# One narrowing operation per slot with its addition on GpSimd, three products held over into a new phase, and the sums' low halves two units later

## The chip, the cores and the metric

One core of a Trainium2 chip runs the whole program. The metric is the device time of one execution in microseconds. The engines are named as in the profile: PE (TensorE) with its weight loads (PEld), DVE (VectorE), ACT (ScalarE), POOL (GpSimd), and SP's queue, which issues every transfer.

## The reference

Windowed attention, then a mixture of eight experts with all experts applied to all tokens, then a two-layer network. Everything is float32.

```python
def reference(q, k, v, w_gate, w1, w2, w_in, w_out):
    x = attention(q, k, v)                    # (2304, 512), banded masks
    P = exp(x @ w_gate - max)                 # (2304, 8)
    for _ in range(8):                        # rows, then columns to equal sums
        P /= P.sum(1, keepdims=True) + 1e-9
        P /= P.sum(0, keepdims=True) + 1e-9
        P *= 2304 / 8
    y = sum(P[:, e:e+1] * (relu(x @ w1[e]) @ w2[e]) for e in range(8))   # hidden 1024
    r = relu(y @ w_in)                        # hidden 2048
    return (r * r) @ w_out
```

## The kernel before, in words

Every float32 operand is split into a high and a low half, and a product is three matmuls: high by high, low operand by high, high by low. The attention fills the first 117 us. After it comes a list of 80 steps of 256 hidden columns each, in four phases: steps 0 to 31 are the experts for a pair of 512-token blocks plus a single 256-token block, steps 32 to 63 the experts for a second pair, steps 64 to 71 the two-layer network for the first pair and the single block, steps 72 to 79 for the second pair. The list `first` holds 0, 32, 64 and 72.

In a step the first layer of the pair is seven units u1 to u7 (`l1_pair`), a seven-product scheme for a two-by-two block product: `blk` slots hold blocks of the weights and `sum` slots hold their sums, made on POOL. A unit is 6 matmuls of 512 columns. u2, u4, u5 and u7 read the sums, u2 as the first, and its third matmul is the first to read their low half. The banks of PSUM are `s`, `pt`, `xt` for the first layer and three `mm` banks for the rest. u5 and u6 write into bank `pt` that ACT has just copied out of (lines 570 and 574); u7 writes into `xt` that DVE has just added from (line 575).

The second layer of step i-1 runs inside step i: `l2_units` makes eight units of 6 matmuls of 512 columns for the pair, and for the single block four units of 6 matmuls of 256 columns (two of 512 in the last network). Each takes an `mm` bank, and DVE adds the bank to `acc` (line 647) before the bank can be used again three units later. `l1_single` makes two more units for the single block.

The order of a step is written by hand: u1 to u4; then second layer, u5, second layer, u6, second layer, u7; then the other five second-layer units; then those of the single block; then the single block's first layer. So a step has 21 units in the first phase and 15 in the second and fourth. At the start of a phase (`first[1:]`) all second-layer units of the old phase run ahead, and u1 to u7 of the new one follow without any between them.

`after(k, f)` puts work on ACT, DVE, POOL or SP's queue behind the unit that is k units from here; every engine takes its work in the order in which it is written. `prep_w(i)` makes the next step's weights in this way: POOL's four additions for the sums at units 0 and 1 (lines 144 to 149), the high half of the sums on ACT at unit 10, their low half (`suml`, line 135) on DVE at unit 12, the low halves of `w2` and `blk` on DVE at units 3 and 5, each followed on SP's queue by the load of the next weights.

The weights of the last network arrive as 64-bit floats. `narrow` turns them into 32-bit floats with bit operations, 32 pieces in all: a load into a buffer `xb`, seven operations on DVE between that buffer and a second one, a store to DRAM. It is a generator, and `narrow_on()` takes it to its next `yield`. It is called from steps 5 to 29 after units 0 and 8, and from steps 33 to 58 after units 0, 5 and 10. The two `xb` buffers are used again by the next piece.

Of the kernel before, what the change touches and what calls it, by code (L numbers as in the profile page):

```python
# [9 lines left out]
F32 = mybir.dt.float32  # L10
# [4 lines left out]
ALU = mybir.AluOpType  # L15
# [26 lines left out]
SCALED = 3  # L42
# [5 lines left out]
def tile_kernel(ctx: ExitStack, tc: tile.TileContext, a):  # L48
    nc = tc.nc
    out = a["out"]  # L50
# [35 lines left out]
    def bank(tag):  # L86
        return psum.tile([128, 512], F32, tag=tag, name=tag, bufs=bufs[tag])
# [9 lines left out]
    sums = wts.tile([128, 4, 256], F32, name="sums")  # L97
# [15 lines left out]
    def load_w(i, which):  # L113
        if i >= len(steps):
            return
        dst = raw1.rearrange("p b c -> p (b c)") if which == 0 else raw2
        nc.sync.dma_start(dst, src_w(i, which))
# [5 lines left out]
    def prep_w(i):  # L123

        out = []
        tt = nc.gpsimd.tensor_tensor
        c = lambda z, k: z[:, k, :]
        flat = lambda z: z.rearrange("p b c -> p (b c)")

        def hi(w, src):  # L130
            return lambda: nc.scalar.copy(w[0], src)  # L131

        def lo(w, src, then=lambda: None):
            def f():
                nc.vector.tensor_tensor(out=w[1], in0=src, in1=w[0].bitcast(F32), op=ALU.subtract)  # L135
                then()

            return f

        if i + 1 < len(steps):  # L140
            w = wset[(i + 1) % 2]

            def s1():
                tt(out=c(sums, 0), in0=c(raw1, 2), in1=c(raw1, 3), op=ALU.add)  # L144
                tt(out=c(sums, 2), in0=c(raw1, 0), in1=c(raw1, 2), op=ALU.subtract)

            def s2():
                tt(out=c(sums, 1), in0=c(sums, 0), in1=c(raw1, 0), op=ALU.subtract)
                tt(out=c(sums, 3), in0=c(raw1, 1), in1=c(sums, 1), op=ALU.subtract)

            out += [(0, s1), (1, s2), (2, hi(w["blk"], flat(raw1)))]
            out += [(5, lo(w["blk"], flat(raw1), lambda: load_w(i + 2, 0)))]
            out += [(10, hi(w["sum"], flat(sums))), (12, lo(w["sum"], flat(sums)))]
        if i >= 0:
            w = wset[i % 2]
            out += [(1, hi(w["w2"], raw2)), (3, lo(w["w2"], raw2, lambda: load_w(i + 1, 1)))]
        return out

    def xb():
        return post[0].tile([128, 2 * T], F32, tag="xb", name="xb", bufs=2)  # L160

    def narrow(which, s, k):

        n = 512
        src = xb().bitcast(I32).rearrange("p (n w) -> p n w", w=2)
        cols = slice(2 * n * k, 2 * n * k + 2 * n)
        nc.sync.dma_start(
            src.rearrange("p n w -> p (n w)"), a["w_in" if which == 0 else "w_out"][s].bitcast(I32)[:, cols]
        )
        yield  # L170
        low, high = src[:, :, 0], src[:, :, 1]
        topf = xb()[:, :n]
        top = topf.bitcast(I32)
        nc.vector.tensor_scalar(
            out=top, in0=high, scalar1=3, scalar2=0x3FFFFFFF,
            op0=ALU.logical_shift_left, op1=ALU.bitwise_and,
        )
        nc.vector.scalar_tensor_tensor(
            out=top, in0=high, scalar=-0x40000000, in1=top, op0=ALU.bitwise_and, op1=ALU.bitwise_or
        )  # L180
        yield
        nc.vector.tensor_scalar(
            out=high, in0=high, scalar1=0x7FFFFFFF, scalar2=None, op0=ALU.bitwise_and
        )
        nc.vector.scalar_tensor_tensor(
            out=topf, in0=high, scalar=float(0x38100000), in1=topf, op0=ALU.is_ge, op1=ALU.mult
        )
        yield
        nc.vector.tensor_scalar(
            out=high, in0=top, scalar1=-0x800000, scalar2=None, op0=ALU.bitwise_and  # L190
        )
        nc.vector.scalar_tensor_tensor(
            out=low.bitcast(F32), in0=low.bitcast(U32), scalar=2.0**-52, in1=high.bitcast(F32),
            op0=ALU.mult, op1=ALU.mult,
        )
        nc.vector.tensor_tensor(out=topf, in0=topf, in1=low.bitcast(F32), op=ALU.add)
        nc.sync.dma_start(w32[which, s, :, n * k:n * k + n], topf)
        yield

# [64 lines left out]
    def load_ps(e):  # L264
        if e < E:
            p = p_t[e] = post[0].tile([128, NSG], F32, tag="ps", name="ps", bufs=1)
            spread(p, e, SINGLE)
# [193 lines left out]
    first = [0, NS1, 2 * NS1, 2 * NS1 + NS2]  # L461

    def phase(i):
        return max(k for k in range(4) if first[k] <= i)

    def pair_of(i):
        return phase(i) % 2
# [16 lines left out]
    def after(k, f):  # L484

        due.setdefault(clock[0] + k, []).append(f)

    def run(u):
        u()
        for f in due.pop(clock[0], []):  # L490
            f()
        clock[0] += 1
# [98 lines left out]
    def l1_single(i):  # L591
        def unit(fc):
            if fc == 0:
                g_t[i, 1] = tuple(
                    post[0].tile([128, FC, NSG], F32R, tag=n, name=n, bufs=1) for n in ("sgh", "sgl")
                )
            gh, gl = g_t[i, 1]
            ps = bank("mm")[:, :NSG]
            hi, lo = wset[i % 2]["blk"]
            k = 0  # L600
            for kc in range(KC):
                c = slice((4 * fc + kc) * 128, (4 * fc + kc) * 128 + 128)
                for w, z in ((hi, xs_hi), (hi, xs_lo), (lo, xs_hi)):
                    nc.tensor.matmul(ps, w[:, c], z[:, kc], start=k == 0, stop=k == 3 * KC - 1)  # L604
                    k += 1
            p = p_t[steps[i][1] // SPE] if steps[i][0] and i >= SCALED else None
            evac_g(i, gh[:, fc], gl[:, fc], ps, p, 0)
            s = steps[i][1]
            if fc == FC - 1 and steps[i][0] and s % SPE == SPE - 1:
                after(1, lambda: load_ps(s // SPE + 1))  # L610

        return [lambda fc=fc: unit(fc) for fc in range(FC)]
# [48 lines left out]
    def operands(i):  # L661

        if phase(i) == 1:
            return new_operands(x_dram)
        t0 = PAIRS[pair_of(i)]
        return new_operands(y_dram[:, :, t0:t0 + 2 * T])

    def operands_single():
        z = xb().rearrange("p (k n) -> p k n", n=NSG)
        nc.sync.dma_start(z, y_dram[:, :, SINGLE:SINGLE + NSG])  # L670
        return single_pieces(z)
# [3 lines left out]
    with tc.manual_schedule():  # L675
# [148 lines left out]
        done = [0]  # L824

        def narrow_on():
            done[0] += 1
            next(narrows, None)

        def settled(i):  # L830

            while done[0] % 4:
                narrow_on()

        for i in range(len(steps) + 1):
            l2 = l2_units(i - 1, 0)
            l2s = l2_units(i - 1, 1)
            if i == len(steps):
                for u in l2 + l2s:
                    run(u)  # L840
                break
            if i in first[1:]:
                for u in l2 + l2s:
                    run(u)
                l2, l2s = [], []
            l1 = l1_pair(i) if i else first_units
            order = l1[:4] if i else l1[2:4]
            for u in l1[4:]:
                order += l2[:1] + [u]
                l2 = l2[1:]  # L850
            order += l2 + l2s
            if i == first[2]:
                l1s = l1_single(i)
                order = l1[:1] + l1s[:1] + l1[1:2] + l1s[1:] + l1[2:]
            elif pair_of(i) == 0:
                order += l1_single(i)
            for k, f in prep_w(i):
                after(min(k, len(order) - 1), f)
            if i + 2 in first[1:]:
                settled(i)  # L860
                for k, f in operands(i + 2):
                    after(len(order) + k, f)
            if i == first[2] - 4:
                for _ in narrows:
                    pass
                for k, f in enumerate(operands_single()):
                    after(8 + 2 * k, f)
            slow = i + 2 in first or i + 1 in first or i in first
            for k, u in enumerate(order):
                run(u)  # L870
                if i < SCALED:
                    next(sink, None)
                if SCALED + 2 <= i < first[2] - 5 and not slow and k in ((0, 8), (0, 5, 10))[pair_of(i)]:
                    narrow_on()
        settle()

# [82 lines left out]
```

## Time and profile before

| | us |
|---|---|
| median of 3 runs | 2045.76 |
| the runs | 2044.92 to 2049.02 |
| the profiled execution | 2052.68 |
| its span from first to last instruction | 2050.9 |
| PE busy | 2017.1 (98%) |
| DVE busy | 1558.3 (76%) |
| ACT busy | 720.4 (35%) |
| POOL busy | 386.6 (19%) |

Matmuls are pipelined and their ends are modelled, so the busy time of PE also covers small gaps. The distance between the starts of two matmuls shows more: 0.23 us at 512 columns and 0.12 us at 256 where nothing is in the way.

### The profile page before, as it was taken

How to read it: one execution, taken by the hardware profiler on the slowest of the kernel's cores; microseconds unless marked ns; L12 is line 12 of the kernel's file. 1: busy time of each engine (PE TensorE's matmuls, PEld its weight loads, DVE VectorE, ACT ScalarE, POOL GpSimd, SP SyncE). 2: the span in 40 equal slices, each digit the busy share in tenths (PEclk: the TensorE clock that was granted, in tenths of full speed). 3: DMA queues.
4: the chain of work that ended last, by engine and by line, in shares of the span. 5: the costliest groups of instructions: out<-in, count | busy, mean ns of one | idle time of the engine just before them, and what ended most of it. 6: DMA issues, size and time to landing. Idle time of an engine off the chain costs nothing.

```text
span 2050.9 us, 28660 instructions
## 1 busy us (share of the span) xinstructions
PE 2017.1 (98%) x11584; PEld 1663.0 (81%) x11584; DVE 1558.3 (76%) x2435; ACT 720.4 (35%) x1149; POOL 386.6 (19%) x416
## 2 busy tenths in 40 slices
PE   9999999999999999999999999999999999999999
PEld 7778888888888888888888888888888878887887
DVE  4766777777777777778888888888887786678676
ACT  3443222223322232223433333333333344344542
POOL 3522311111011111111311212121211231123120
PEclk8899999999999999999999999999999999999999
DMA  8512121222212121213222322323221231112111
GB/s 279 177 65 61 52 57 57 62 65 62 65 50 61 56 61 47 70 57 98 103 93 87 87 85 71 97 78 98 82 86 59 75 111 42 39 54 103 62 42 52
DMA packets 71509, 159.35 MB, mean 78 GB/s; under 512 B 6336, under 2 KB 33104, under 8 KB 71376
## 3 DMA queue, kind: packets, MB, share of 16 engines
q1 hardware_dynamic: 71376, 157.52, 23.8%
q8 instruction: 91, 1.49, 0.3%
q14 instruction: 42, 0.34, 0.1%
HBM read 137.49 MB, written 20.00 MB: 77 GB/s over the span
## 4 chain that ended last, share of the span: by engine, by line
PE 87%; DVE 10%; ACT 2%; issue 1%; POOL 0%; ACTq 0%; DVEq 0%; POOLq 0%
PE mm L635 42%; PE pt L477 16%; PE s L477 10%; PE xt L477 9%; PE mm L604 5%; DVE acc L647 3%; PE xt L349 2%; DVE gl L511 2%; DVE g L525 1%; DVE suml L135 1%; PE mm L752 1%; PE s L297 1%; PE pt L334 1%; DVE x_lo L212 1%; DVE s L584 1%
## 5 line engine op out<-in xcount | busy, mean ns | idle before, releaser
L647 DVE TENSOR_TENSOR acc<-mm,acc 128x512 f32<-128x512 f32 x746 | 473.2, 642 | 188.4 <-PE mm L635 184.4
L635 PE MATMUL mm<-gl,w2h 128*128 128x512 f32 x1024 | 403.3, 394 | 0.0
L635 PE MATMUL mm<-gh,w2h 128*128 128x512 f32 x1024 | 402.3, 393 | 0.8 <-DVE acc L647 0.7
L635 PE MATMUL mm<-gh,w2l 128*128 128x512 f32 x1024 | 402.8, 393 | 0.0
L533 ACT CAST gh<-g 128x512 fp32r<-128x512 f32 x308 | 191.5, 622 | 592.8 <-DVE g L525 592.6
L144 POOL TENSOR_TENSOR sums<-raw 128x256 f32<-128x256 f32 x80 | 66.2, 827 | 1466.7 <-DVE suml L135 1423.8
L635 PEld LDWEIGHTS mm<-gh,w2h 128*128 128x128 f32 x1024 | 192.4, 188 | 46.8 <-DVE acc L647 1.6
L635 PEld LDWEIGHTS mm<-gl,w2h 128*128 128x128 f32 x1024 | 192.3, 188 | 43.9
L635 PEld LDWEIGHTS mm<-gh,w2l 128*128 128x128 f32 x1024 | 192.3, 188 | 43.7
L511 DVE TENSOR_TENSOR gl<-g,gh 128x512 fp32r<-128x512 f32 x308 | 223.8, 731 | 0.9 <-ACT gh L533 0.9
L525 DVE SCALAR_TENSOR_TENSOR g<-s,pp 128x512 f32<-128x512 f32 x183 | 128.8, 704 | 111.6 <-PE s L477 109.4
L477 PE MATMUL pt<-x_hi,sumh 128*128 128x512 f32 x320 | 126.4, 395 | 3.7 <-ACT s L570 3.7
L477 PE MATMUL s<-x_hi,blkh 128*128 128x512 f32 x320 | 126.3, 395 | 1.0 <-ACT pt L558 1.0
L477 PE MATMUL xt<-x_hi,sumh 128*128 128x512 f32 x320 | 126.6, 396 | 0.0
L477 PE MATMUL xt<-x_lo,sumh 128*128 128x512 f32 x320 | 126.0, 394 | 0.0
L477 PE MATMUL pt<-x_lo,sumh 128*128 128x512 f32 x320 | 125.9, 393 | 0.0
L477 PE MATMUL xt<-x_hi,suml 128*128 128x512 f32 x320 | 125.9, 393 | 0.0
L477 PE MATMUL pt<-x_hi,suml 128*128 128x512 f32 x320 | 125.8, 393 | 0.0
L477 PE MATMUL s<-x_lo,blkh 128*128 128x512 f32 x320 | 125.8, 393 | 0.0
L477 PE MATMUL s<-x_hi,blkl 128*128 128x512 f32 x320 | 125.5, 392 | 0.0
L135 DVE TENSOR_TENSOR w2l<-raw,w2h 128x1024 fp32r<-128x1024 f32 x80 | 100.7, 1259 | 14.9 <-ACT w2h L131 14.9
L533 ACT CAST sgh<-g 128x256 fp32r<-128x256 f32 x74 | 29.9, 406 | 219.0 <-DVE g L525 219.0
(151 smaller groups left out, 3970.3 us busy)
## 6 DMA issues: line engine op xcount, KB each, us to landing
raw<-in_w SPq DMA_DIRECT2D x128, 512.0 KB, 3.5
raw<-w SPq DMA_DIRECT2D x32, 512.0 KB, 3.4
v<-in_v SPq DMA_DIRECT2D x24, 384.0 KB, 3.9
pp<-p_dram SPq DMA_DIRECT2D x32, 256.0 KB, 5.6
xb<-in_w_in SPq DMA_DIRECT2D x16, 512.0 KB, 4.7
w<-xb SPq DMA_DIRECT2D x32, 256.0 KB, 2.3
xb<-in_w_out SPq DMA_DIRECT2D x16, 512.0 KB, 4.7
k<-in_k SPq DMA_DIRECT2D x24, 224.0 KB, 4.6
```

Of the source, the lines that this page charges most:

```text
L135: nc.vector.tensor_tensor(out=w[1], in0=src, in1=w[0].bitcast(F32), op=ALU.subtract)
L144: tt(out=c(sums, 0), in0=c(raw1, 2), in1=c(raw1, 3), op=ALU.add)
L212: return lambda: nc.vector.tensor_tensor(out=x_lo[:, k, j], in0=z, in1=x_hi[:, k, j].bitcast(F32), op=ALU.subtract)
L297: nc.tensor.matmul(ps[QB * head:QB * head + QB, 2 * (g % 3) + g // 3, :], qt[rows, pr, g * QB:g * QB + QB], kt[rows, pr, g * QB:g * QB + K ...
L349: nc.tensor.matmul(xt[D * h:D * h + D, pr, c * QB:c * QB + QB], vt[keys, c, head * D:head * D + D], pt[keys, c * 128 + head * QB:c * 128 + ...
L477: nc.tensor.matmul(ps, w[:, c], z[:, x, j], start=start and k == 0, stop=stop and k == 5, skip_group_check=True)
L511: nc.vector.tensor_tensor(out=glo, in0=z, in1=ghi.bitcast(F32), op=ALU.subtract)
L525: nc.vector.scalar_tensor_tensor(out=held["g"], in0=src, scalar=0.0, in1=held["r"], op0=ALU.max, op1=ALU.mult)
L533: after(k + 1, lambda: nc.scalar.copy(ghi, held["g"]))
L604: nc.tensor.matmul(ps, w[:, c], z[:, kc], start=k == 0, stop=k == 3 * KC - 1)
L635: nc.tensor.matmul(ps, lhsT, rhs, start=k == 0, stop=k == 3 * FC - 1)
L647: nc.vector.tensor_tensor(out=dst, in0=ps, in1=dst, op=ALU.add)
```

## The change

- The low half of the sums is put on DVE behind unit 14 of a step, not 12. Where a step has only 15 units that is its last one.
- `narrow` yields after each operation, so one call is one operation, and a piece is eight calls instead of four: the load; six operations on DVE, one a call; the addition with the store.
- The last of its seven operations, the addition, goes to POOL.
- `narrow_on()` is called five times a step: after units 0, 1, 2, 7 and 20 in the first phase, after 0, 1, 2, 7 and 13 in the second.
- At the start of a phase the last three second-layer units of the old phase are kept back and put between u5, u6 and u7 of the new one.
- In step 0 the two units of the single block go between u4, u5 and u6.

```diff
-            out += [(10, hi(w["sum"], flat(sums))), (12, lo(w["sum"], flat(sums)))]
+            out += [(10, hi(w["sum"], flat(sums))), (14, lo(w["sum"], flat(sums)))]
...
             op0=ALU.logical_shift_left, op1=ALU.bitwise_and,
         )
+        yield
         nc.vector.scalar_tensor_tensor(
...
             out=high, in0=high, scalar1=0x7FFFFFFF, scalar2=None, op0=ALU.bitwise_and
         )
+        yield
...
             out=high, in0=top, scalar1=-0x800000, scalar2=None, op0=ALU.bitwise_and
         )
+        yield
...
-        nc.vector.tensor_tensor(out=topf, in0=topf, in1=low.bitcast(F32), op=ALU.add)
+        yield
+        nc.gpsimd.tensor_tensor(out=topf, in0=topf, in1=low.bitcast(F32), op=ALU.add)
         nc.sync.dma_start(w32[which, s, :, n * k:n * k + n], topf)
...
-            while done[0] % 4:
+            while done[0] % 8:
...
+            ahead = []
             if i in first[1:]:
-                for u in l2 + l2s:
-                    run(u)
-                l2, l2s = [], []
+                ahead, l2, l2s = l2[:-3] + l2s, l2[-3:], []
             l1 = l1_pair(i) if i else first_units
-            order = l1[:4] if i else l1[2:4]
-            for u in l1[4:]:
-                order += l2[:1] + [u]
-                l2 = l2[1:]
-            order += l2 + l2s
-            if i == first[2]:
-                l1s = l1_single(i)
-                order = l1[:1] + l1s[:1] + l1[1:2] + l1s[1:] + l1[2:]
-            elif pair_of(i) == 0:
-                order += l1_single(i)
+            l1s = l1_single(i) if pair_of(i) == 0 else []
+            if i == 0:
+                order = l1[2:4] + l1s[:1] + l1[4:5] + l1s[1:] + l1[5:]
+            elif i == first[2]:
+                order = l1[:1] + l1s[:1] + l1[1:2] + l1s[1:] + l1[2:4]
+            else:
+                order = l1[:4]
+            if i:
+                for u in l1[4:]:
+                    order += l2[:1] + [u]
+                    l2 = l2[1:]
+                order += l2 + l2s
+                if i != first[2]:
+                    order += l1s
+            for u in ahead:
+                run(u)
...
-                if SCALED + 2 <= i < first[2] - 5 and not slow and k in ((0, 8), (0, 5, 10))[pair_of(i)]:
+                if SCALED + 2 <= i < first[2] - 5 and not slow and k in ((0, 1, 2, 7, 20), (0, 1, 2, 7, 13))[pair_of(i)]:
                     narrow_on()
```

## Rows read from the trace of the kernel before

**Rows 1.** Busy time of each engine, page of the whole execution.
```profile
PE 2017.1 (98%) x11584; PEld 1663.0 (81%) x11584; DVE 1558.3 (76%) x2435; ACT 720.4 (35%) x1149; POOL 386.6 (19%) x416
```

**Rows 2.** Busy time by stretch: steps 11, 12, 30, 41 and 43, u1 to u1.
```profile
407.59:434.27 26.68, 26.68 (x140) 22.61 (x139) 18.98 (x31) 7.91 (x12) 3.31 (x4) 1.00 0.16 50
434.27:461.82 27.55, 27.00 (x140) 22.72 (x139) 20.60 (x34) 7.91 (x12) 3.31 (x4) 1.00 0.23 73
922.60:949.07 26.47, 26.47 (x140) 22.60 (x139) 21.06 (x34) 7.91 (x12) 3.33 (x4) 1.00 0.30 100
...
1170.30:1191.12 20.82, 20.82 (x91) 16.91 (x90) 17.77 (x27) 7.05 (x10) 3.35 (x5) 1.00 0.22 70
1211.92:1232.91 20.99, 20.99 (x91) 16.83 (x90) 18.90 (x29) 7.05 (x10) 4.58 (x5) 1.00 0.31 101
```

**Rows 3.** Waits of PE, whole execution: total us, times, longest.
```profile
PE mm L635 <- DVE acc L647: 11.3, 31, 1.4
...
PE pt L477 <- ACT s L570: 3.7, 6, 0.7
PE pt L477 <- ACT s L574: 2.4, 4, 0.7
```

**Rows 4.** Timeline of PE in step 32: start, us; u6 after u5.
```profile
999.53 0.39 PE L477 MATMUL pt<-x_hi,suml 128*128 128x512 f32 x1
1000.60 0.50 PE L477 MATMUL pt<-x_hi,blkh 128*128 128x512 f32 x1 [0.68 <-ACT s L574]
1000.93 0.39 PE L477 MATMUL pt<-x_lo,blkh 128*128 128x512 f32 x1
```

**Rows 5.** Timeline of PE in step 12: first matmuls of single-block units 16, 17, 18.
```profile
456.11 0.38 PE L635 MATMUL mm<-sgh,w2h 128*128 128x256 f32 x1 [0.17 <-DVE acc L647]
...
457.48 0.39 PE L635 MATMUL mm<-sgh,w2h 128*128 128x256 f32 x1 [0.38 <-DVE acc L647]
...
458.29 0.28 PE L635 MATMUL mm<-sgh,w2h 128*128 128x256 f32 x1
```

**Rows 6.** Timeline of DVE in steps 12 and 61, and 62 beginning.
```profile
454.24 1.22 DVE L135 TENSOR_TENSOR suml<-sums,sumh 128x1024 fp32r<-128x1024 f32 x1
...
1605.31 0.69 DVE L647 TENSOR_TENSOR acc<-mm,acc 128x512 f32<-128x512 f32 x1
1605.91 1.22 DVE L135 TENSOR_TENSOR suml<-sums,sumh 128x1024 fp32r<-128x1024 f32 x1
...
1607.65 0.85 DVE L511 TENSOR_TENSOR gl<-g,gh 128x512 fp32r<-128x512 f32 x1
```

**Rows 7.** Timeline of PE, steps 61 and 62: start of unit 13, u1, u2's third matmul.
```profile
1605.11 0.40 PE L635 MATMUL mm<-gh,w2h 128*128 128x512 f32 x1
...
1607.91 0.40 PE L477 MATMUL s<-x_hi,blkh 128*128 128x512 f32 x1
...
1609.77 0.40 PE L477 MATMUL xt<-x_hi,suml 128*128 128x512 f32 x1
```

**Rows 8.** Groups by form (busy us, mean ns); POOL's timeline, step 61.
```profile
L196 DVE TENSOR_TENSOR xb<-xb 128x512 f32<-128x512 f32 x32 | 24.7, 773 | 1.1
...
L144 POOL TENSOR_TENSOR sums<-raw 128x256 f32<-128x256 f32 x80 | 66.2, 827 | 1466.7 <-DVE suml L135 1423.8 <-DMA raw<-in_w 42.9
L206 POOL TENSOR_TENSOR xb<-xb 128x512 f32<-128x512 f32 x24 | 33.9, 1412 | 67.6 <-DVE x_lo L212 66.6
...
1607.90 1.19 POOL L145 TENSOR_TENSOR sums<-raw 128x256 f32<-128x256 f32 x1
```

**Rows 9.** Transfers: issues, KB each, median us to landing.
```profile
xb<-in_w_in SPq DMA_DIRECT2D x16, 512.0 KB, 4.7
```

**Rows 10.** Timeline of DVE in step 45: three operations back to back.
```profile
1261.98 1.22 DVE L135 TENSOR_TENSOR blkl<-raw,blkh 128x1024 fp32r<-128x1024 f32 x1
1263.11 0.42 DVE L174 TENSOR_SCALAR xb<-xb 128x512 int32<-128x512 int32 x1
1263.57 0.69 DVE L178 SCALAR_TENSOR_TENSOR xb<-xb 128x512 int32<-128x512 int32 x1
```

## Prediction

> **What bounds the kernel now.** The page says PE: busy 98% of the span, DVE 76% [rows 1]. An average hides where the rest goes, so the table by stretch comes next. In the second phase a step takes 20.8 us, one in four 21.0, and PE is busy in all of it [rows 2]: no edit can gain there but what a few short stalls hold. In the first phase steps alternate: 26.68 us, 27.55 us, and in step 30, which has no narrowing, 26.47 us [rows 2]. The work on PE is the same, so 0.2 or 1.1 us of a step is waiting. The list of PE's waits names it: 11.3 us in 31 waits for DVE's addition out of an `mm` bank, and 6.1 us in 10 waits for ACT's copies out of `pt` [rows 3]. The timeline gives the price of such a wait: u6 starts 1.07 us after the matmul before it and the next one 0.33 us on, where two times 0.23 would do (2.80 us for twelve [rows 7]). The loss is 0.94 us for an idle time of 0.68, so 0.26 on top of each wait, 0.10 of it the slower restart [rows 4].
>
> Why the waits are there: in step 12 the single block's units come every 0.71 us, and DVE, with 2 us of narrowing behind unit 8 and the sums' low half (1.22 us) behind unit 12, is late with the banks of units 13 and 14. Unit 17 starts 1.37 us after unit 16 in place of 0.71 [rows 5, 6].
>
> **The change part by part.** Gains first.
>
> *Narrowing one operation at a time, first phase.* None of the five spots lies between unit 7 and the last unit. The 12 heavier steps (27.55) lose their DVE queue and would come to 26.47: 12 x 1.08 = 13.0 us; the 13 lighter ones 13 x 0.21 = 2.7.
>
> *The sums' low half at unit 14, first phase.* It now stands between the additions of units 14 and 15. Count from the start of unit 15. DVE's addition starts 0.20 us after the unit's end (1605.11 to 1605.31 [rows 6, 7]) and the next operation follows 0.60 later, so the low half runs from 0.80, the next operation 1.13 later (the 1024-column row [rows 10]) at 1.93, and bank 15 is free at about 2.40. Unit 18 needs that bank at 3 x 0.71 = 2.13. That costs 0.27 + 0.10 = 0.37 us in each of 27 steps: 10.0. The two lines together: 13.0 + 2.7 - 10.0 = 5.7. Some old stalls behind unit 12, before the phase changes, get shorter because the additions of units 13 and 14 now come 1.1 us sooner (steps 3, 31, 63, 71; the longest of their waits is 1.4 [rows 3]); I take 3 us, bounds 0 and 5.
>
> *Three products kept for the new phase.* u5 and u6 then have a unit of 1.4 us in front of each, longer than the 0.94 they lose. Of the 6 and 4 waits in rows 3, three phases hold one of each kind: 3 x 2 x 0.94 = 5.6 us. The other four share 6.1 - 6 x 0.68 = 2.0 us of idle time; two of them are in step 0, where single-block units now stand between: half of it and 0.1 a wait, 1.2. What could take this back is DVE, which in the run ahead has fewer units to catch up in: 0.4.
>
> *Second phase, narrowing.* One step in four loses 0.2 us to it now [rows 2]: six steps, 1.2.
>
> Gains together: 5.7 + 3 + 5.6 + 1.2 - 0.4 + 1.2 = 16.3 us.
>
> *The sums' low half, second and fourth phase.* Here a step has 15 units, so unit 14 is the last and the low half stands behind its addition. From u1 of the next step: addition at 0.20, low half at 0.80, ready at 0.80 + 1.22 = 2.02. PE's first matmul that reads it, u2's third, now starts 1609.77 - 1607.91 = 1.86 after u1 [rows 7]. Before the change it was ready at 1605.91 + 1.22 = 1607.13, 2.6 us ahead of that matmul [rows 6]. Now u2 is held by 0.16 + 0.10 = about 0.3 us a step. And one narrowing operation now stands behind unit 13: unit 13's addition starts at -1.20, `gl` follows at -0.60 and ends its turn at 0.00, and then 0.46 [rows 10] or 0.60 us of narrowing come before the addition of unit 14, so that it starts 0.26 or 0.40 later than 0.20. Of eight calls three are the short kind, three the long kind and two not on DVE: (3 x 0.56 + 3 x 0.70 + 2 x 0.3) / 8 = 0.55 us. The 26 steps with narrowing cost 14.3, the 4 after them and the 6 of the fourth phase 0.3 each, 3.0. Sum 17.3 us. No row shows PE waiting for this tile; from below the price is nothing, if the weights come through sooner than DVE's row ends, from above 0.8 us in each of 36 steps, 29. I take 17.3, since it is made of rows of the same instructions.
>
> *Load, addition and first operation of a piece.* A piece has eight calls and a step five, so in a cycle of eight steps the addition falls once behind unit 0, with the next load behind unit 1 and the first operation behind unit 2 (steps 8, 16, 24 and 36, 44, 52). POOL has the sums' first two additions in front of it. In the second phase those start when the low half is read, 2.4 us after u1, and take 1.7 us; the addition about 1.4 [rows 8]; only then is the buffer free, and the load lands 4.7 us later [rows 9], at 10.2. DVE reaches the operation at about 5 and stands, since it takes its work in order. Behind it wait the low half of `w2` (1.13), two additions and two further operations (0.60 each) and the low half of `blk` (1.13): with its own 0.46 the addition into u7's bank ends at about 15.4, where u7 is due at 9 x 1.40 + 0.7 = 13.3. Cost 2.1 + 0.1, with the store's issue ahead of the load some 2.4 us, in three steps: 7. Bounds 0 (the load lands in time) and 3 x 5.2, the whole wait, 16. In the first phase the sums are long made at u1, the load lands near 7.5, and u7 is held by about 0.2: 0.6.
>
> *The addition on POOL.* It leaves 32 x 0.77 = 25 us of DVE's time [rows 8], off PE's path but for the stalls counted above. POOL needs 1.41 us for the nearest form, 1.8 times as long [rows 8], and is idle four fifths of the time [rows 1]. POOL's work lengthens some of DVE's operations: `gl`, at 1607.65 beside POOL's sums, took 0.85 us, where another operation of 512 columns takes 0.69 [rows 6, 8]. In the second phase the sums on POOL move some 2 us later, beside DVE's low halves, but the addition for u7 has some 1.7 us to spare there (without the wait above, its queue of two narrowing operations, product, third operation and the rest ends near 11.6 by the same durations, against 13.3), so I put this at nothing; it costs up to 0.3 us in each of 30 steps, 9, when that cover is gone.
>
> Sum: 16.3 - 17.3 - 7 - 0.6 = -8.6, that is some 8 us slower. Against the profiled execution's own 2052.68 (span 2050.9 and 1.8 around it) that is 2060.7. The median of the runs shown lies 6.9 us below that execution, so the forecast for a median is 2045.76 + 8 = 2054 us.
>
> **The rivals.**
>
> The low half in time (faster). If PE is not held at u2, 17.3 us fall away: 2036.7, 9 us faster than before. For it: the 0.16 us of lateness is the difference of two numbers near 2, and one turn of DVE that is 0.2 us shorter undoes it. Against: the narrowing behind unit 13 adds more than that in six steps of eight. It decides at a mean hold under 0.13 us a step, where the loss here falls below 5 us and the whole comes out ahead by 4. Chance 0.17.
>
> The load not in DVE's way: 7.6 us fall away, 2046.4, no change that a measurement shows. For it: SP's queue runs ahead of PE and could issue earlier. Against: the buffer is freed only by POOL's addition. With smaller slips of the same size elsewhere, chance 0.23.
>
> POOL in DVE's way: each of 30 steps of the second phase pays the 0.3 us, 9 us more, 2063. For it: 0.85 against 0.69 us for one operation beside POOL, and several stand in the queue before u7. Against: the 1.7 us to spare. Chance 0.12. The Trainium skill has the mechanism in GPSIMD Engine Reference, section 1 (Specifications): GpSimd's SBUF interfaces are shared with VectorE, with contention for VectorE's instructions with two SBUF inputs. By that rule, the trace agrees for `gl`, which reads two.
>
> **How the numbers follow.** My forecast has a chance of 0.48 and its own range 2048 to 2061. A measurement of this kernel tells some 0.2%, 4.1 us, from no change. Slower by more: 0.40 of the forecast and 0.12 of POOL's rival, with a little of the second one, 0.54. Within: 0.24. Faster: the first rival, and 0.05 of the others where the first phase gains its full 15.7 instead of 5.7: 0.22. The range takes in the first rival's upper half and POOL's: 2037 to 2065.
>
> **What would show it.** In the timeline of the second phase, step 62's u2 has its third matmul behind a wait of PE's weight load for `suml`, and a step with narrowing is some 0.5 us over 20.8. Steps 36, 44 and 52 have DVE idle for some 5 us until `xb<-in_w_in` lands, with PE late at u7. First-phase steps are all near 26.8. PE's waits for lines 570 and 574 shrink to almost nothing. The forecast is wrong if steps of the second phase stay at 20.8, or if first-phase steps fall to 26.5 and more is gained at the phases than 7 us. PE's pace between 0.227 and 0.233 us a matmul, which I took as unchanged, could also move the end by a few us.

## The result, and the profile after

The changed kernel takes 2059.99 us (median of 4 runs, 2057.24 to 2061.84), the kernel before 2045.34 us beside it: a ratio of 1.007, 95% interval 1.0058 to 1.0083. It is 14.65 us slower. The forecast was 2054, range 2037 to 2065.

The busy times say little. DVE has 32 instructions and 17 us less to do, POOL 32 and 30 us more, PE the same work ([rows 1] for before):

```profile
PE 2020.6 (98%) x11584; PEld 1657.9 (80%) x11584; DVE 1541.4 (75%) x2403; ACT 720.8 (35%) x1149; POOL 417.0 (20%) x448
```

The windows of the same five steps as in [rows 2] show what went where:

```profile
402.17:429.09 26.92, 26.79 (x140) 22.67 (x139) 19.32 (x32) 7.91 (x12) 4.29 (x5) 1.00 0.27 79
429.09:455.93 26.84, 26.74 (x140) 22.66 (x139) 20.52 (x34) 7.91 (x12) 4.18 (x5) 1.00 0.24 74
912.93:939.77 26.84, 26.74 (x141) 22.66 (x140) 21.34 (x32) 7.91 (x12) 8.28 (x9) 1.00 0.31 98
...
1166.50:1187.74 21.24, 21.14 (x91) 16.83 (x90) 16.42 (x25) 7.06 (x10) 2.94 (x4) 1.00 0.15 50
1209.24:1230.61 21.37, 21.09 (x91) 16.83 (x90) 17.99 (x27) 7.06 (x10) 3.38 (x4) 1.00 0.21 62
```

Steps 11 and 12 were 26.68 and 27.55 and are now nearly alike; step 30, which has no narrowing, went from 26.47 up to 26.84, so that rise is not narrowing's. The steps of the second phase from step 35 on are all longer. Step 41, which follows a step without a DVE operation of the narrowing behind its unit 13, is longer by 0.42; step 43, which follows one with such an operation, by 0.38 (it had a narrowing stall before, which is gone).

By stage, u1 to u1, in us. The first two columns are the two profiles; the others belong to the experiments below. Each column is one profiled execution. In steps 0–2 and 31–32 profiles of kernels with the same instructions there differ by 1.4 to 1.6 us; that is TensorE's clock (last section).

| steps | before | after | after − before | low half at 12 | other spots | before, 14 | three kept | narrowing alone | last kernel |
|---|---|---|---|---|---|---|---|---|---|
| 0–2 | 72.8 | 76.0 | +3.2 | 72.4 | 75.6 | 74.3 | 72.7 | 72.7 | 73.9 |
| 3–30 | 758.8 | 753.6 | −5.2 | 744.6 | 753.0 | 754.7 | 758.6 | 744.9 | 742.8 |
| 31–32 | 54.4 | 53.0 | −1.4 | 54.4 | 53.0 | 54.3 | 54.4 | 54.8 | 53.0 |
| 33–62 | 625.2 | 648.4 | +23.2 | 625.8 | 633.9 | 638.3 | 625.2 | 625.2 | 623.9 |
| 63–65 | 75.4 | 74.3 | −1.1 | 73.8 | 74.3 | 75.7 | 73.9 | 75.4 | 73.8 |
| 66–70 | 131.6 | 131.6 | 0 | 131.6 | 131.6 | 131.6 | 131.6 | 131.6 | 131.6 |
| 71–73 | 75.7 | 71.8 | −3.9 | 72.7 | 71.8 | 74.8 | 72.7 | 75.6 | 71.8 |
| 74–79, to PE's end | 135.4 | 137.3 | +1.9 | 135.4 | 137.3 | 137.2 | 135.4 | 135.4 | 135.4 |

The stages add up to +16.7. The spans differ by 9.2 only, because u1 of step 0 starts at 117.45 in the profiled execution of before and at 110.13 in that of after (that stage is not changed, and this is about the 6.9 by which the profiled execution of before lay above its median). What lies between 16.7 and the 14.65 of the medians is within the spread of single executions.

PE's waits, total, times and longest: of the `mm` banks (11.3 in 31 [rows 3]) little is left, and of `pt` one wait. In their place stand `suml`, `s` (the addition out of u7's bank) and a longer `scs`.

```profile
PE xt L481 <- DVE suml L135: 6.6, 18, 0.5
...
PE xt L481 <- DVE s L579: 5.8, 5, 1.8
PE mm L439 <- DVE scs L433: 3.2, 2, 2.0
...
PE mm L639 <- DVE acc L651: 1.8, 6, 0.5
...
PE pt L481 <- ACT s L574: 1.3, 1, 1.3
```

The same view of the weight loads counts more of them (37 for `suml` against 18 on PE): a load that waits while the matmul in front of it still runs leaves PE no idle time of its own:

```profile
PEld xt L481 <- DVE suml L135: 23.7, 37, 0.9
PEld mm L639 <- DVE acc L651: 14.4, 40, 0.7
```

Filtered by stage, 29 of the 37 for `suml` lie in steps 33 to 62, 3 in steps 63 to 65 and 71 to 73, and 5 behind u1 of step 74; of the 40 for `acc`, 28 lie in steps 3 to 30, once a step, as forecast for the unit behind the low half (the other 12 at the phases' changes and in step 0 to 2).

Step 62 is the step of [rows 6, 7], and the prediction's count can be read off it. PE, its weight load and DVE:

```profile
1620.13 0.40 PE L481 MATMUL s<-x_hi,blkh 128*128 128x512 f32 x1
...
1621.76 0.39 PE L481 MATMUL xt<-x_lo,sumh 128*128 128x512 f32 x1
1622.21 0.50 PE L481 MATMUL xt<-x_hi,suml 128*128 128x512 f32 x1
1622.54 0.40 PE L481 MATMUL xt<-x_hi,sumh 128*128 128x512 f32 x1
...
1622.20 0.19 PEld L481 LDWEIGHTS xt<-x_hi,suml 128*128 128x128 f32 x1 [0.49 <-DVE suml L135]
...
1620.33 0.69 DVE L651 TENSOR_TENSOR acc<-mm,acc 128x512 f32<-128x512 f32 x1
...
1620.94 1.22 DVE L135 TENSOR_TENSOR suml<-sums,sumh 128x1024 fp32r<-128x1024 f32 x1
```

u1 is at 1620.13. The addition of unit 14 follows at 0.20, the low half at 0.81, and it is done at 1620.94 + 1.22 = 1622.16, which is 2.03 after u1 (the count gave 2.02). The weight load goes 0.04 later. From u2's second matmul to its third is 0.45 us and from the third to the next 0.33, where 2 × 0.23 would do: 0.32 lost, which the prediction had at 0.3.

### The profile page after: what moved, and what is told of

Same layout as the page of the kernel before. It is cut to its first block, busy times and chain, and to the rows that moved or that the text cites. A ratio compares the mean times of both kernels' runs of the same rounds, so it can differ in the third digit from the quotient of the medians.

```text
span 2060.1 us, 28704 instructions
## 1 busy us (share of the span) xinstructions
PE 2020.6 (98%) x11584; PEld 1657.9 (80%) x11584; DVE 1541.4 (75%) x2403; ACT 720.8 (35%) x1149; POOL 417.0 (20%) x448
## 4 chain that ended last, share of the span: by engine, by line
PE 83%; DVE 12%; issue 1%; ACT 1%; DMA 1%; POOL 0%; SPq 0%; DVEq 0%; ACTq 0%; POOLq 0%
PE mm L639 41%; PE pt L481 15%; PE xt L481 10%; PE s L481 8%; PE mm L608 5%; DVE acc L651 4%; DVE suml L135 4%; PE xt L353 2%; DVE gl L515 1%; DVE x_lo L216 1%; DMA xb<-in_w_out 1%; PE mm L756 1%; PE s L301 1%; DVE g L529 1%; PE pt L338 1%
## 5 line engine op out<-in xcount | busy, mean ns | idle before, releaser
L515 DVE TENSOR_TENSOR gl<-g,gh 128x512 fp32r<-128x512 f32 x308 | 212.2, 693 | 0.0
L481 PE MATMUL xt<-x_hi,suml 128*128 128x512 f32 x320 | 130.4, 407 | 8.1 <-DVE suml L135 6.6
```

Of the source, the lines that this page charges most:

```text
L481: nc.tensor.matmul(ps, w[:, c], z[:, x, j], start=start and k == 0, stop=stop and k == 5, skip_group_check=True)
L515: nc.vector.tensor_tensor(out=glo, in0=z, in1=ghi.bitcast(F32), op=ALU.subtract)
```

## Experiments

Each kernel changes few things in the kernel after or before. Its stages are in the table above where it has a column there.

**The low half back at unit 12, all else as changed.**

```diff
-            out += [(10, hi(w["sum"], flat(sums))), (14, lo(w["sum"], flat(sums)))]
+            out += [(10, hi(w["sum"], flat(sums))), (12, lo(w["sum"], flat(sums)))]
```

> The changed kernel with the sums' low half back at unit 12. My theory: it is the low half at unit 14 that costs most. Second-phase steps come back from 21.1 to 21.5 us to 20.8, the three steps 36, 44 and 52 keep their hold at u7; first-phase steps go from 26.84 and 26.92 to about 26.47. Some 18 + 11 = 29 us less than the changed kernel's 2060: 2031. Rival, the narrowing spots alone cost the second phase its time: second-phase steps stay above 21, the first phase stays or gets worse, 2050 or more.

Measured: 2025.65 us, ratio to before 0.9901 (0.9883 to 0.9919). First-phase steps are 26.47 and 26.53, second-phase steps 20.79 to 20.80. PE's waits have no `suml` row left, `acc` has seven, mostly at the phases' changes, and `s` (u7's bank, line 579) less than a third:

```profile
PE mm L639 <- DVE acc L651: 4.6, 7, 1.4
...
PE xt L481 <- DVE s L579: 1.5, 4, 0.6
```

The sums' unit alone decides the sign: without it the change is 20 us faster, with it 15 us slower. It came out 5 us below the expectation, because the load's wait shrank as well: steps 36, 44 and 52 take 21.25, 21.26 and 21.68, held by 0.46, 0.47 and 0.89 in place of some 9 in all. With the low half earlier POOL has the old sums free sooner, makes the next ones and then the piece's addition sooner, and the load follows. DVE stood 2.68 us for it in step 36, against 4.28 with the low half at 14:

```profile
1052.13 0.43 DVE L174 TENSOR_SCALAR xb<-xb 128x512 int32<-128x512 int32 x1 [2.68 <-DMA xb<-in_w_out]
```

**Other spots for the narrowing,** with the low half left at 14: load, addition and first operation lie farther apart, and none lies behind unit 13.

```diff
-                if SCALED + 2 <= i < first[2] - 5 and not slow and k in ((0, 1, 2, 7, 20), (0, 1, 2, 7, 13))[pair_of(i)]:
+                if SCALED + 2 <= i < first[2] - 5 and not slow and k in ((0, 2, 4, 7, 20), (0, 3, 6, 9, 12))[pair_of(i)]:
```

> The changed kernel with other spots for narrowing, units 0, 2, 4, 7, 20 in the first phase and 0, 3, 6, 9, 12 in the second; sums' low half stays at unit 14. My theory: the hold at u7 in steps 36, 44, 52 is gone, with the half-speed matmuls after it (some 10 us), and no narrowing stands before the last addition, so all second-phase steps cost the 0.3 us of the steps without narrowing (21.1): 26 x 0.2 = 5 us. 2045. Rival, the load is not what DVE stands for: the three steps stay long, 2055.

Measured: 2047.55 us over 10 runs, ratio 1.0002 (0.9989 to 1.0016). From step 35 on all second-phase steps are 21.10 or 21.20, also 36, 44 and 52. Steps 33 to 62 lost 14.5 us of the 23.2: 9.1 is the hold in those three steps, the other 5.4 the operation behind unit 13. The 8.7 that remain over the kernel before, and the 1.2 that the kernel before lost there to narrowing, make 9.9 in 30 steps: 0.33 a step, the low half's own price.

**The piece's addition on DVE, all else as changed.**

```diff
-        nc.gpsimd.tensor_tensor(out=topf, in0=topf, in1=low.bitcast(F32), op=ALU.add)
+        nc.vector.tensor_tensor(out=topf, in0=topf, in1=low.bitcast(F32), op=ALU.add)
```

> The changed kernel with the addition of the narrowing back on DVE, all else as changed. My theory: the load in steps 36, 44 and 52 waits for an addition that stands behind POOL's sums; on DVE the addition comes sooner by some 2 us, so DVE stands about 2 us instead of 4.3, u7 is held by less than 1 us and the matmuls keep their pace: some 7 us less, 2053. Rival, the load's own time is what counts: DVE stands 4 us as before and the time is unchanged at 2060.

Measured: 2060.96 us, ratio 1.0069 (1.0052 to 1.0086), the same as with POOL. It didn't come out at the 2053 expected. The hold at steps 36 and 44 is gone (21.49 each; 22.13 in step 52), 8.4 us in the three, but others came: steps 13, 21 and 29 took 28.20, 28.59 and 28.42, 4.4 more than in the kernel after, and 41, 49 and 57 took 21.75, 22.07 and 21.75, 1.9 more. DVE's waits for the loads, total, times and longest, are more, not fewer; the first fence is the kernel after, the second this one:

```profile
DVE xb L174 <- DMA xb<-in_w_out: 14.4, 5, 4.3
DVE xb L174 <- DMA xb<-in_w_in: 8.6, 4, 4.3
```

```profile
DVE xb L174 <- DMA xb<-in_w_out: 23.1, 8, 4.3
DVE xb L174 <- DMA xb<-in_w_in: 11.7, 4, 3.9
```

On DVE the addition sits at its own spot in the order, so the buffer comes free only there; POOL, whose queue is its own, does it as soon as the sixth operation is done, often a spot ahead. In step 13 the addition, the load's issue and the first operation stand like this:

```profile
458.54 0.68 DVE L200 TENSOR_TENSOR xb<-xb 128x512 f32<-128x512 f32 x1
...
459.62 0.44 SPq L167 DMA_DIRECT2D xb<-in_w_in  x1
...
463.81 0.43 DVE L174 TENSOR_SCALAR xb<-xb 128x512 int32<-128x512 int32 x1 [3.92 <-DMA xb<-in_w_in]
```

So the wait for the load belongs to the spots, and POOL makes it late only in the steps in which its queue is full of sums.

**The low half at 14, in the kernel before.**

```diff
-            out += [(10, hi(w["sum"], flat(sums))), (12, lo(w["sum"], flat(sums)))]
+            out += [(10, hi(w["sum"], flat(sums))), (14, lo(w["sum"], flat(sums)))]
```

> The kernel before with one edit: the sums' low half at unit 14 instead of 12. My theory: second- and fourth-phase steps rise by about 0.3 us each, 36 of them, 11 us; in the first phase the steps of 26.68 rise by 0.2 and those of 27.55 fall by up to 0.5, as narrowing behind unit 8 still fills DVE: -3 us. 2045 + 8 = 2053. Rival, PE is held at u2 only together with the narrowing behind unit 13: second-phase steps stay at 20.8, 2043.

Measured: 2057.93 us, ratio 1.0055 (1.004 to 1.007), +12 where +8 was expected. Steps 3 to 30 gain 4.1 us, steps 0 to 2 lose 1.5, steps 33 to 62 13.1, the fourth phase 1.8. Second-phase steps run 21.1, 21.4, 21.1, 21.73 by turns: a whole group of narrowing behind unit 10 delays the low half still at unit 14, which the expectation left out.

**Three products kept for the new phase alone** (step 0 keeps its old order here).

```diff
-                for u in l2 + l2s:
-                    run(u)
-                l2, l2s = [], []
+                ahead, l2, l2s = l2[:-3] + l2s, l2[-3:], []
```

> The kernel before with one edit: three second-layer units kept back at the start of a phase (step 0 as before). My theory, from the changed kernel with the sums at unit 12: u5 and u6 no longer wait in steps 32, 64 and 72, but in the run ahead DVE's queue holds PE up by about as much at step 31; net 0, -1.6 and -3 us in the three places, 2041. Rival, the full price of the waits, 5.6, and of u3 one step later, 2.4, is gained: 2037.

Measured: 2040.57 us, ratio 0.997 (0.9957 to 0.9983), −5.8 us. By stage 0 at steps 31–32, −1.5 at 63–65, −3.0 at 71–73, which is 4.5. The 0 at 31–32 is not the products' own: the clock fell there in this execution and took back 1.4 (under "The products kept" below).

**Narrowing one operation at a time alone,** with POOL's addition and the new spots; sums at 12, no products kept.

```diff
+        yield
-        nc.vector.tensor_tensor(out=topf, in0=topf, in1=low.bitcast(F32), op=ALU.add)
+        nc.gpsimd.tensor_tensor(out=topf, in0=topf, in1=low.bitcast(F32), op=ALU.add)
...
-            while done[0] % 4:
+            while done[0] % 8:
...
-                if SCALED + 2 <= i < first[2] - 5 and not slow and k in ((0, 8), (0, 5, 10))[pair_of(i)]:
+                if SCALED + 2 <= i < first[2] - 5 and not slow and k in ((0, 1, 2, 7, 20), (0, 1, 2, 7, 13))[pair_of(i)]:
```

> The kernel before with one edit: narrowing as in the changed kernel (one operation a call, addition on POOL, its spots), nothing else. My theory: first-phase steps 26.5 us throughout, 14 us less; second-phase steps 20.8 with three of some 21.3 to 21.7: 2032. With the three kept products it adds up to the changed kernel with the sums at unit 12, 2026. Rival, POOL's addition lengthens DVE's operations by enough to hold PE: second-phase steps above 21 us, 2036 or more.

Measured: 2031.38 us, ratio 0.9937 (0.9917 to 0.9957): −13.9 us in steps 3 to 30 and 0.0 in 33 to 62, where the old stalls of the narrowing (1.2) go and the load holds steps 36, 44 and 52 by 0.6, 0.3 and 0.5. With the 5.8 of the products kept this makes some 21, and the two together (the first experiment) came to 20: the parts add up, and the third, the sums' unit, turns the sum.

**Sums at 12 and the other spots together.**

```diff
-            out += [(10, hi(w["sum"], flat(sums))), (14, lo(w["sum"], flat(sums)))]
+            out += [(10, hi(w["sum"], flat(sums))), (12, lo(w["sum"], flat(sums)))]
...
-                if SCALED + 2 <= i < first[2] - 5 and not slow and k in ((0, 1, 2, 7, 20), (0, 1, 2, 7, 13))[pair_of(i)]:
+                if SCALED + 2 <= i < first[2] - 5 and not slow and k in ((0, 2, 4, 7, 20), (0, 3, 6, 9, 12))[pair_of(i)]:
```

> The changed kernel with the sums at unit 12 and the other spots for narrowing (0, 2, 4, 7, 20 and 0, 3, 6, 9, 12). My theory: steps 8, 36, 44 and 52 lose their last hold, 0.9 + 0.5 + 0.5 + 0.9 us: 2023. Rival, an operation behind unit 12 between the low half and the additions holds PE up again in the second phase: no gain on 2026.

Measured: 2024.54 us, ratio 0.9893 (0.9876 to 0.9909). The hold is gone in each of its places (step 8 takes 26.46, steps 36, 44 and 52 take 20.79). In the medians that is 1.1 us on the first experiment, less than the intervals tell apart. The profiles show −1.0 in steps 3 to 30 and −1.9 in 33 to 62, which is the 2.8 expected. They also show −1.4 in 31–32 and +1.6 in 0–2 (53.0 and 74.0), but the edit changes nothing in those steps: there the matmuls ran at the lower clock in one of the two executions and not in the other.

**The same, with the low half at 14 in steps 3, 31 and 71 only,** where it runs ahead of a phase's change.

```diff
-            out += [(10, hi(w["sum"], flat(sums))), (12, lo(w["sum"], flat(sums)))]
+            out += [(10, hi(w["sum"], flat(sums))), (14 if i in (3, 31, 71) else 12, lo(w["sum"], flat(sums)))]
```

> As the last one, but with the sums' low half at unit 14 in steps 3, 31 and 71 alone, where it stood in front of late additions and no u2 comes right behind: 0.8 + 1.4 + 0.9 us less, 2020. Rival, those stalls are only moved to the run ahead: 2023.

Measured: 2021.55 us, ratio 0.9877 (0.9862 to 0.9892), 1.2% faster than before and 1.9% than after (2021.55 / 2059.99). Its interval overlaps that of the last one. In the profiles the edit gains 0.9 in step 3 and 0.9 in step 71, as expected, and nothing in step 31 (39.10 and 39.08), where 1.4 were expected. Of PE's waits that this case turned on there are left 2.3 us in six waits for `acc` (longest 0.7), one of 1.6 for `scs` and one of 1.2 for ACT's line 574.

## Why the prediction came out as it did

It had the direction, and the place of most of the loss; the time lies inside its range, 6 us over its forecast. Term against stage (after − before, us; the prediction's terms put together by stage from its own numbers):

| stage | predicted | measured |
|---|---|---|
| 0–2 | −1.2 | +3.2 |
| 3–30: narrowing −15.7, low half +10.0, load +0.6 | −5.1 | −5.2 |
| phases' changes: products −5.6 + 0.4, old stalls −3 | −8.2 | −6.4 |
| 33–62: low half 14.3 + 1.2, load 7, narrowing −1.2 | +21.3 | +23.2 |
| 74–79: low half | +1.8 | +1.9 |
| sum | +8.6 | +16.7 |

Of the 8.1 by which the stages are over the forecast, some 4.8 is a thing that no term had: three times, in steps 1, 36 and 52, eight matmuls ran at TensorE's lower clock behind a wait, 1.6 us each.

**First phase.** Narrowing alone gained 13.9 of the 15.7. The low half in this phase, the kernel after against that with the sums at 12, costs 753.6 − 744.6 = 9.0 of the 10.0: 9.8 in steps 4 to 30, less 0.8 in step 3, which is one of the prediction's old stalls. "All near 26.8" is seen: 26.84 and 26.92.

**The low half in the second and fourth phase.** Right in place, cause and size: 0.3 to 0.4 us a step over the kernel before, 0.6 to 0.7 where an operation stands behind unit 13 of the step before (steps of 21.37 to 21.50, against 21.10 to 21.24). Leaving out the hold below and the 1.2 that narrowing gave back, 23.2 − 9.1 + 1.2 = 15.3 against the 15.5 predicted. The first rival, that the tile is in time, is refuted by the `suml` row with 37 waits, and by the experiment that takes that row away with the unit.

**The load's wait.** The chain was right, the price 9.1 instead of 7. Steps 36, 44 and 52 took 25.14, 23.22 and 25.19; over 21.5 for a step of their kind that is 3.64, 1.72 and 3.69. In step 36, DVE, then POOL, then SP's queue, then PE:

```profile
1057.23 1.21 DVE L135 TENSOR_TENSOR suml<-sums,sumh 128x1024 fp32r<-128x1024 f32 x1
...
1066.10 0.43 DVE L174 TENSOR_SCALAR xb<-xb 128x512 int32<-128x512 int32 x1 [4.28 <-DMA xb<-in_w_out]
1066.44 1.22 DVE L135 TENSOR_TENSOR w2l<-raw,w2h 128x1024 fp32r<-128x1024 f32 x1
...
1070.51 0.68 DVE L579 TENSOR_TENSOR s<-xt,s 128x512 f32<-128x512 f32 x1
...
1058.57 0.74 POOL L144 TENSOR_TENSOR sums<-raw 128x256 f32<-128x256 f32 x1 [18.14 <-DVE suml L135]
...
1059.97 1.32 POOL L200 TENSOR_TENSOR xb<-xb 128x512 f32<-128x512 f32 x1
...
1061.32 0.33 SPq L201 DMA_DIRECT2D w<-xb  x1
1061.74 0.38 SPq L167 DMA_DIRECT2D xb<-in_w_out  x1
...
1071.25 0.50 PE L481 MATMUL xt<-x_hi,sumh 128*128 128x512 f32 x1 [1.80 <-DVE s L579]
...
1072.17 0.63 PE L481 MATMUL xt<-x_hi,sumh 128*128 128x512 f32 x1
1072.60 0.63 PE L481 MATMUL xt<-x_lo,sumh 128*128 128x512 f32 x1
```

With u1 at 1056.02 the order is: `suml` done at 1058.44, POOL's two sums, the addition until 1061.29, the store and then the load's issue at 1061.74, DVE's first operation at 1066.10 (10.08 after u1; the prediction had 10.2), the addition into u7's bank done at 1071.19 (15.17 after u1; it had 15.4). PE then waits 1.80 us; the count had 2.1 for it and 2.4 a step with the restart and the store. What was left out comes behind the wait: some eight matmuls stand 0.43 us apart in place of 0.23, as the last two lines show, which adds 8 × 0.2 = 1.6 us in steps 36 and 52 and nothing in 44. Without these the three holds come to 9.1 − 3.2 = 5.9: the wait itself was put somewhat too high, and the slow matmuls, for which the prediction had no term, more than made up for it. The second rival, that the load is not in DVE's way, did not come in the kernel as changed; with the sums at 12 it nearly does (holds of 0.46 to 0.89).

**Step 0.** The one term with the wrong sign: −1.2 was forecast, +3.2 came. The two waits for `pt` did go, as forecast; what the prediction left out is what DVE would do with the new order. A wait of PE for `scs` (line 433), 1.0 us long in the kernel before, is now 1.96 us, and there is a second one of 1.28. PE, then DVE, then POOL in step 1:

```profile
131.96 0.39 PE L439 MATMUL mm<-scs,xb 128*128 128x8 f32 x2 [1.96 <-DVE scs L433]
...
125.20 1.23 DVE L135 TENSOR_TENSOR suml<-sums,sumh 128x1024 fp32r<-128x1024 f32 x1 [0.69 <-ACT sumh L131]
126.34 0.69 DVE L511 SCALAR_TENSOR_TENSOR gl<-s,gh 128x512 fp32r<-128x512 f32 x1
...
127.54 0.68 DVE L588 TENSOR_TENSOR s<-xt,s 128x512 f32<-128x512 f32 x1
...
128.57 0.74 DVE L443 TENSOR_SCALAR sct<-sct 128x8 f32<-128x8 f32 x1
129.34 0.81 DVE L444 TENSOR_TENSOR ptile<-ptile,sct 128x144 f32<-128x144 f32 x1
...
131.49 0.41 DVE L433 TENSOR_REDUCE scs<-ptile 128x8 f32<-128x144 f32 x1
...
128.54 0.74 POOL L145 TENSOR_TENSOR sums<-raw 128x256 f32<-128x256 f32 x1
129.24 0.74 POOL L148 TENSOR_TENSOR sums<-sums,raw 128x256 f32<-128x256 f32 x1
```

The low half, two `gl` and a product's addition now stand in one row in front of the normalising chain that ends in `scs`. The runs split the loss. The new order with the low half at 12 has no wait for `pt`, but one of 1.58 for `scs` in place of 1.0, and gains 0.4 (72.4), not 1.2. The low half at 14 in the old order brings the second wait, 1.28, and +1.5 (74.3). Both together make +3.2: besides the sum of the two, 1.1, the matmuls behind the longer first wait run 0.43 us apart, eight of them, 8 × 0.2 = 1.6 us, and the wait itself is 1.96 in place of 1.58. These last two do not come from the low half's unit. The last two kernels above have the order and the low half at 12, the same instructions in these steps as the first experiment, and in their executions the matmuls are slow too (74.0 and 73.9 against 72.4, behind waits of 1.60 and 1.59). The kernel with the other spots, in these steps the same as the kernel after, has the first wait at 1.58. Why it was 1.96 here, the last section shows.

**The products kept.** 5.6 less 0.4 was forecast for them and 3 for the old stalls; the stages gave 6.4 together, and the products alone 4.5. At step 31 it went as forecast: the two waits for `pt` cost 1.87 us with their restarts, and they are gone; in the run ahead PE loses 2.9 us to DVE in place of 2.5. That is −1.4, and it is what the kernel after, the one with the other spots and the last one show (53.0). The products alone, and the first experiment, show 0 there (54.4). Both have a wait of 1.37 us for `acc` in step 31, and behind it some 16 matmuls of 256 columns ran 0.21 us apart in place of 0.12. The kernel with the sums at 12 and the other spots has the same instructions and a wait of 1.39 there, and kept the full clock. The windows are the four us behind it, the first experiment and then that kernel; the number after POOL's is the granted clock:

```profile
952.40:956.40 4.00, 4.00 (x24) 4.00 (x23) 4.00 (x6) 1.60 (x3) 2.89 (x2) 0.57 0.00 0
```

```profile
951.40:955.40 4.00, 4.00 (x36) 4.00 (x36) 4.00 (x6) 1.59 (x3) 2.93 (x2) 1.00 0.00 1
```

Without that the products come to 4.5 + 1.4 = 5.9. A new wait for ACT's copy out of `pt` in step 64 is in this already, 1.2 us there and 1.3 in the kernel after (line 574). Of the old stalls less came than the 3 forecast: 0.9 in step 3 (counted in the row of steps 3–30) and 0.9 in step 71, from the last kernel against the one before it, and nothing in step 31.

**The addition on POOL.** Put at nothing, with POOL in DVE's way as the third rival at 0.3 us a step. Not seen: with the sums at 12 a second-phase step is 20.79 to 20.80, as before [rows 2], and `gl` as a group takes 693 ns after and 731 before. The addition itself takes 1.73 us on the average of 32, more than the 1.41 of the nearest form, and no one waits for that difference but the load.

## What to carry to other kernels

The same move of two units can be harmless for the reader in one phase and late in another: behind unit 14 the low half still had six units and u1 ahead of its reader in a step of 21 units, and u1 alone in a step of 15. Count from the reader in each phase on its own, and weigh a gain of few steps against a small wait in all of them. An instruction that depends on a DMA, put into the order of an engine that works in sequence, is worth as many spots of distance as load, buffer release and issue take together; with that distance it cost nothing here, without it 9 us in three steps. Where a change has several parts, the time of the whole hides them: two of these three gained 20 us, and the third took back 34 (2059.99 − 2025.65). Nor is the price of a part its own: alone, in the kernel before, the third cost 12.

## What the hardware showed that was not expected

**TensorE's clock can fall after a wait of under 2 us.** The windows below are of the kernel after: step 36 before and in the slow matmuls and behind them, step 52, step 44, and step 1. The column after POOL's is the granted clock. It goes from full (2.4 GHz) to the lower level (1.2 GHz; a window that holds both lies between) after idle times of 1.80 (step 36), 1.82 (step 52) and 1.96 us (step 1), and it is back some 4 to 5 us after the wait; in step 44, after 1.45 us, it stays full.

```profile
1069.00:1071.00 2.00, 0.44 (x2) 0.00 (x1) 2.00 (x3) 0.00 (x0) 0.00 (x0) 1.00 0.58 229
1071.00:1075.00 4.00, 3.75 (x10) 2.98 (x11) 3.88 (x7) 1.86 (x3) 0.00 (x0) 0.61 0.35 133
1075.00:1081.00 6.00, 6.00 (x27) 4.90 (x27) 4.28 (x7) 0.94 (x2) 0.00 (x0) 0.97 0.00 0
...
1420.00:1424.00 4.00, 4.00 (x13) 3.09 (x12) 3.36 (x6) 1.57 (x2) 0.00 (x0) 0.57 0.06 23
1240.00:1252.00 12.00, 10.55 (x46) 8.30 (x45) 11.62 (x18) 3.08 (x5) 0.00 (x0) 1.00 0.27 87
132.00:137.00 5.00, 5.00 (x16) 4.03 (x17) 4.72 (x13) 0.76 (x2) 0.00 (x0) 0.66 0.30 105
```

The idle time alone doesn't decide. After the wait of 1.58 us in step 1 the clock of the five us behind it is 0.66 in the kernel with the other spots and 1.00 in the one with the low half at 12; the last two kernels, with the instructions of the latter in these steps and waits of 1.60 and 1.59, have 0.66 again. The wait of 1.37 to 1.39 us in step 31 stands in five of the kernels, and the matmuls behind it were slow in two of them, at full speed in three. What else decides was not tried. So a difference of 1.4 to 1.6 us between two profiles can be the clock alone. In step 36 the slow matmuls cost 1.6 us beside a wait of 1.80: the view of waits showed about half of the loss.

**Some operations of DVE stand until POOL's are done.** In the rows of step 1 above, line 444 reads two tiles from SBUF; it takes 0.31 us where POOL is idle. There it took 0.81 and ended 0.17 us after the POOL addition beside which it began (130.15 against 129.98). Line 443 (one tile, 8 columns) took 0.74 in place of 0.17: it began at 128.57, 0.03 us behind the start of a POOL addition, and ended at 129.31, 0.03 us behind its end. In the kernel with the low half at 12 line 443 began 0.03 us before that addition and took 0.17:

```profile
128.84 0.17 DVE L443 TENSOR_SCALAR sct<-sct 128x8 f32<-128x8 f32 x1
...
128.87 0.74 POOL L145 TENSOR_TENSOR sums<-raw 128x256 f32<-128x256 f32 x1
```

Line 444 began beside the same addition there and took 0.73. With the other spots it went as in that kernel. So the 0.4 us by which the wait for `scs` in step 1 is longer in the kernel after goes with a shift of 0.06 us between two starts. The Trainium skill has a contention of this kind in GPSIMD Engine Reference, section 1 (Specifications): the two engines share their SBUF interfaces, and VectorE's instructions in a two-port mode or with two SBUF inputs contend with GpSimd's. By that rule, the trace agrees for line 444, which reads two tiles from SBUF; for line 443, which reads one, no row here shows the mode.
